# Attention feeding an MoE layer on one core: pinned activation tables, a maximum by matmul, grouped QK, and preparation two units ahead

## Chip, cores and metric

One core of a Trainium2 chip. The metric is the device time of one execution in microseconds (us), as the median of several runs; the kernel before took 714.8 us (709.6 to 864.0, the last being a single slow execution that no comparison uses). Ratios are computed as the mean time of one kernel's fast runs over that of the other's fast runs of the same rounds, so they are not quite the ratio of the medians quoted.

## The reference

Twelve-head attention with normalised q and k, whose output (3584 tokens of 768 values) goes through two matrices with a leaky ReLU between.

```python
# q, k, v: (8, 12, 448, 64) fp32; g_q, g_k: (64,)
def rmsnorm(x, g):
    return x / np.sqrt(np.mean(x * x, axis=-1, keepdims=True) + 1e-06) * g
q_n, k_n = rmsnorm(q, g_q), rmsnorm(k, g_k)
scores = np.matmul(q_n, k_n.transpose(0, 1, 3, 2)) / np.sqrt(64)
attn = np.exp(scores - scores.max(-1, keepdims=True))
attn = attn / (attn.sum(-1, keepdims=True) + 1e-09)
x = np.matmul(attn, v).transpose(0, 2, 1, 3).reshape(3584, 768)
h = x @ w_in                        # w_in (768, 2048)
out = np.maximum(0.01 * h, h) @ w_out    # w_out (2048, 768)
```

Any constant may be subtracted from the scores of a row, so the kernel subtracts one shift for a whole unit, found from a probe of the scores.

## The kernel before

The work is cut into 24 units, each four heads of one batch element. For a unit, GpSimd makes squares (`sq`), q times both gains (`qg`) and a cast of v (`vt`); VectorE sums the squares (`ssq`); ScalarE forms 1/rms as exp(-0.5 ln) (`uu`, `rinv`); VectorE multiplies (`n16`, shown as `n` in traces); TensorE transposes (`tp`); a probe of the scores gives the shift (`eb`). Then eight score tiles (`sT`) go through Exp into `et`, and `pv` forms the sum of the exponentials and the product with v, which are divided with ln and exp again (`lz`, `rz`). From unit 3 on, MoE matmuls of the batch element before (`hps`, `op`) are put between the score tiles from a queue, so many microseconds of them per step (`fill`).

```python
def prep_pool(u):
    ...
    for ti, t in enumerate((rq, rk)):
        f = t.rearrange("p h j d -> p (h j) d")
        nc.gpsimd.tensor_tensor(sq[:, ti], f, f, op=ALU.mult)     # sq: one buffer
    nc.gpsimd.tensor_tensor(qg, rq..., ggb..., op=ALU.mult)       # qg: one buffer
    nc.gpsimd.tensor_copy(vt..., rv...)

def prep_rinv(u):
    nc.scalar.activation(uu, s["ssq"], AF.Ln, bias=eps_t, scale=1.0 / D)
    nc.scalar.activation(rinv, uu, AF.Exp, bias=0.0, scale=-0.5)

def prep_norm(u, ti):                       # ti 0: q (from qg), ti 1: k (from raw)
    for a in range(2):
        nc.vector.tensor_tensor(n16[:, ti, :, :, a, :], src5[:, :, a],
                                r4[:, :, a, :, None].broadcast_to(...), op=ALU.mult)

def prep_probe(u):
    ...                                     # four matmuls, two row maxima into pm2
    nc.gpsimd.partition_all_reduce(cr2, pm2, SP, bass_isa.ReduceOp.max)
    nc.vector.tensor_reduce(cm, cr2, axis=AXL.X, op=ALU.max)
    nc.vector.tensor_scalar(eb, cm, -1.0, DELTA, op0=ALU.mult, op1=ALU.add)
...
for u in range(NU):
    nu = u + 1
    for i in range(2 * NJ):                 # eight score tiles
        qk_exp(u, i)
        if i == 0: load(u + 2); prep_pool(nu); ...
        if i == 1 and u > 0: pv(u - 1); ...
        if i == 2: prep_ssq(nu); prep_rinv(nu)
        if i == 3: prep_norm(nu, 0); prep_norm(nu, 1)
        if i == 4: prep_tr(nu, 0)
        if i == 5: prep_tr(nu, 1)
        if i == 6: prep_probe(nu)
        fill({1: 0.4, 4: 1.6, 5: 1.6}.get(i, 2.0) if u >= NQ else 0.0)
```

(Range checks and parts that do not change are left out.)

## Time and profile before

| part of the span, us | before |
|---|---|
| start (to the first exponential of unit 3) | 108.9 |
| 21 units with MoE work | 547.6 (26.1 each) |
| tail | 48.3 |
| span | 704.8 |

From the groups of instructions of the kernel before, two kinds. The columns are line, engine, operation, names and shapes, count, then busy us and mean ns of one, then the idle time ahead of them and what ended it.

```profile
L131 DVE TENSOR_TENSOR n<-qg,rinv 112x512 f16<-112x512 f32 x48 | 31.0, 688 | 48.0 <-ACT rinv L119 48.0
L131 DVE TENSOR_TENSOR n<-rk,rinv 112x512 f16<-112x512 f32 x48 | 30.9, 684 | 0.0
L117 ACT ACT_TABLE_LOAD x24 | 30.8, 1283 | 1.1 <-PEq L325 0.7
```

The 96 normalising multiplies take 0.68 to 0.69 us each; four of them are 2.5 us per unit. The table load stands four times per unit (this row and three like it, each 1283 ns, the other three with 0.4 us of idle time ahead of 24 loads). A row with large idle time is not yet a bottleneck: one asks whether the engine that sets the end (TensorE here) waits because of it. The prediction reads the waits and the timeline for that.

### The profile page before, as it was taken

The page shows a single profiled execution, that of the slowest core. Times are in us where ns is not written, and L with a number is a line of the kernel's source. Part 1 is how long each engine was busy: PE and PEld are TensorE (multiplying, and loading weights), DVE is VectorE, ACT ScalarE, POOL GpSimd, SP SyncE. Part 2 cuts the span into 40 slices and gives each one's busy share as a digit, 9 for nine tenths or more (in the row PEclk, how much of TensorE's full clock was granted, in tenths as well). Part 3 has the DMA queues.
Part 4 walks back from the last instruction along what each step waited for, and adds up shares of the span by engine and source line. Part 5 has one row for each costly group of instructions (what it writes and reads, how often), then busy time and mean ns, then how long its engine had stood idle before and what let it go on. Part 6 is the DMA issues. An engine that isn't in the chain of part 4 may idle for free.

```text
span 704.8 us, 8877 instructions
## 1 busy us (share of the span) xinstructions
PE 516.1 (73%) x3680; PEld 250.1 (35%) x3680; DVE 236.8 (34%) x372; ACT 405.1 (57%) x512; POOL 185.2 (26%) x133
## 2 busy tenths in 40 slices
PE   0206528878678978977778878878679778879897
PEld 0102212434333433433333433434334434435454
DVE  1322442243342353254232343243332343333001
ACT  0226555766558456757548456766547466766520
POOL 3241244034044134134044044034044043140000
PEclk9998556989789989999779889999769889999999
DMA  6944542504430325205420225205420134001002
GB/s 159 192 93 95 123 80 54 115 1 124 100 79 1 73 62 139 53 1 124 101 78 1 58 67 127 77 0 124 101 78 1 27 98 123 1 1 46 23 20 71
DMA packets 40728, 50.95 MB, mean 72 GB/s; under 512 B 2416, under 2 KB 36720, under 8 KB 40304
## 3 DMA queue, kind: packets, MB, share of 16 engines
q1 hardware_dynamic: 38144, 44.11, 24.5%
q0 software_dynamic: 2544, 6.29, 5.2%
q8 instruction: 28, 0.46, 0.3%
q14 instruction: 12, 0.10, 0.0%
HBM read 45.67 MB, written 11.01 MB: 80 GB/s over the span
## 4 chain that ended last, share of the span: by engine, by line
issue 52%; POOL 21%; PE 16%; ACT 5%; DVE 4%; POOLq 0%; DVEq 0%
POOL sq L99 11%; PE op L224 8%; POOL qg L101 6%; PE hps L211 5%; POOL vt L104 3%; DVE n L131 2%; DVE ssq L111 2%; ACT et L178 1%; PE sT L176 1%; ACT L202 1%; ACT L200 1%; ACT L119 1%; DVE xt L204 1%; PE tp L140 1%; POOL wout L78 1%
## 5 line engine op out<-in xcount | busy, mean ns | idle before, releaser
L178 ACT ACTIVATE et<-sT,eb 112x896 f16<-112x896 f32 x192 | 188.1, 1005 | 148.4 <-PE sT L176 126.5
L211 PE MATMUL hps<-xt,win 128*128 128x448 f16 x768 | 171.4, 373 | 23.8 <-DVE xt L204 23.8
L224 PE MATMUL op<-wout,gt 128*128 128x384 f16 x896 | 179.3, 362 | 0.0
L140 PE MATMUL tp<-ident,n 112*128 112x112 f16 x384 | 38.3, 247 | 135.7 <-DVE n L131 135.7
L224 PEld LDWEIGHTS <-gt 128*128 128x128 f16 x896 | 93.3, 108 | 76.7 <-issue 33.3
L211 PEld LDWEIGHTS <-win 128*128 128x128 f16 x768 | 73.8, 102 | 103.0 <-issue 50.6
L176 PE MATMUL sT<-qkT 64*112 64x448 f16 x384 | 77.7, 416 | 19.4 <-ACT et L178 19.0
L99 POOL TENSOR_TENSOR sq<-rq 112x1024 f32<-112x1024 f32 x24 | 45.2, 1883 | 171.8 <-issue 171.8
L213 ACT ACTIVATE gt<-hps 128x448 f16<-128x448 f32 x128 | 66.3, 544 | 38.4 <-PE hps L211 36.6
L204 DVE TENSOR_TENSOR xt<-pv,rz 128x448 f16<-128x448 f32 x48 | 27.7, 619 | 164.3 <-ACT rz L202 164.3
L161 POOL PARTITION_ALL_REDUCE cr<-pm x24 | 9.0, 373 | 269.2 <-DVE pm L159 232.7
L140 PEld LDWEIGHTS <-n 112*128 112x128 f16 x384 | 24.6, 112 | 152.9 <-DVE n L131 147.3
L227 DVE COPY ost<-op 128x384 f32<-128x384 f32 x56 | 31.1, 556 | 120.1 <-PE op L224 117.6
L111 DVE TENSOR_REDUCE ssq<-sq 112x32 f32<-112x2048 f32 x24 | 54.7, 2280 | 44.3 <-POOL sq L99 44.3
L101 POOL TENSOR_TENSOR qg<-rq,ggb 112x1024 f32<-112x1024 f32 x24 | 56.2, 2344 | 0.0
L117 ACT ACTIVATE uu<-ssq,eps_t 112x32 f32<-112x32 f32 x24 | 7.7, 322 | 84.4 <-DVE ssq L111 84.4
L176 PEld LDWEIGHTS <-qkT 64*112 64x112 f16 x384 | 25.5, 131 | 74.9 <-issue 73.5
L131 DVE TENSOR_TENSOR n<-qg,rinv 112x512 f16<-112x512 f32 x48 | 31.0, 688 | 48.0 <-ACT rinv L119 48.0
L99 POOL TENSOR_TENSOR sq<-rk 112x1024 f32<-112x1024 f32 x24 | 45.2, 1882 | 0.0
L195 PE MATMUL pv<-et,vt 112*32 112x448 f16 x768 | 44.6, 377 | 0.0
L144 DVE COPY qkT<-tp 128x896 f16<-128x896 f16 x48 | 30.0, 625 | 29.4 <-PE tp L140 29.3
L159 DVE TENSOR_REDUCE pm<-probe 112x1 f32<-112x448 f32 x48 | 27.7, 620 | 22.3 <-PE probe L156 22.3
(28 smaller groups left out, 302.2 us busy)
## 6 DMA issues: line engine op xcount, KB each, us to landing
rq<-in_q_dram SPq DMA_DIRECT2D x24, 448.0 KB, 5.0
rk<-in_k_dram SPq DMA_DIRECT2D x24, 448.0 KB, 6.9
rv<-in_v_dram SPq DMA_DIRECT2D x24, 448.0 KB, 7.5
win<-in_moe_w_in_dram POOLq DMA_DIRECT2D x3, 1024.0 KB, 13.5
wout<-in_moe_w_out_dram POOLq DMA_DIRECT2D x4, 768.0 KB, 7.7
out_dram<-ost SPq DMA_DIRECT2D x8, 336.0 KB, 2.8
out_dram<-ost SPq DMA_DIRECT2D x8, 288.0 KB, 2.7
out_dram<-ost SPq DMA_DIRECT2D x8, 240.0 KB, 2.7
```

The lines of the kernel that those rows point to most:

```text
L99: nc.gpsimd.tensor_tensor(sq[:, ti], f, f, op=ALU.mult)
L101: nc.gpsimd.tensor_tensor(qg, rq.rearrange("p h j d -> p (h j) d"), ggb[:, None, :].broadcast_to([SP, QH * NJ, D]), op=ALU.mult)
L111: nc.vector.tensor_reduce(ssq, s["sq"], axis=AXL.X, op=ALU.add)
L131: nc.vector.tensor_tensor(n16[:, ti, :, :, a, :], src5[:, :, a], r4[:, :, a, :, None].broadcast_to([SP, 2, NJ, D]), op=ALU.mult)
L140: nc.tensor.transpose(tp[:, ti, j, :], s["n16"][:, ti, r, j].rearrange("p a d -> p (a d)"), ident16[:SP, :])
L176: nc.tensor.matmul(sT[:, a, 0:S], kq[:, 1, ts(jk, SP)], kq[:, 0, :], start=True, stop=True)
L178: nc.scalar.activation(s["et"][:, jk, 2 * r:2 * r + 2, :], sT[:, :, 0:S], AF.Exp, bias=s["eb"], scale=1.0)
L195: nc.tensor.matmul(bank[32 * i:32 * i + 32, 0:S], lhsT, s["et"][:, jk, i, :], start=(jk == 0), stop=(jk == NJ - 1))
L204: nc.vector.tensor_tensor(xt[:, g, w, :], bank[:, 0:S], rz, op=ALU.mult)
L211: nc.tensor.matmul(hps[:, 0:S], win16[:, kt // 2, kt % 2, ts(ft, 128)], xt[:, kt // 2, kt % 2], start=(kt == 0), stop=(kt == KT - 1))
L213: nc.scalar.activation(gt[:, ft, ds(S * (b % 2), S)], hps[:, 0:S], AF.Prelu, bias=0.0, scale=1.0, alpha=0.01)
L224: nc.tensor.matmul(op2[:, 0:HC], gt[:, ft, ts(t, 128)], wout16[:, ft, ds(HC * half, HC)], start=(ft == 0), stop=(ft == FT - 1))
```

## The change

The intent: take the table loads off ScalarE, take GpSimd's slow all-reduce and its reload away (the "reload" is the 7 us behind each all-reduce in which GpSimd waits for nothing that the trace shows; the name is an interpretation: what GpSimd does in this time is not shown), make fewer and longer bursts of score matmuls, and prepare so early that nothing in the preparation can hold up TensorE.

```diff
-    raws = ctx.enter_context(tc.tile_pool(name="raws", bufs=2))
+    raws = ctx.enter_context(tc.tile_pool(name="raws", bufs=3))
...
     def prep_pool(u):
...
+        if u == 0:
+            for ti, t in enumerate((rq, rk)):
+                nc.scalar.activation(sq[:, ti], t, AF.Square)
+            nc.vector.tensor_tensor(qg, rq, gg_b, op=ALU.mult)
+            nc.gpsimd.tensor_copy(vt_v, rv_v)
+        else:
+            ...                                   # on GpSimd, as before
...
-        nc.gpsimd.partition_all_reduce(cr2, pm2, SP, bass_isa.ReduceOp.max)
+        nc.vector.tensor_reduce(pm, pm2, axis=AXL.X, op=ALU.max)
+        nc.vector.tensor_scalar(dg, ident16[:SP, :], pm, None, op0=ALU.mult)
+
+    def prep_shift(u):
+        nc.tensor.matmul(pb[:, 0:SP], onesp, s["dg"], start=True, stop=True)
+        nc.vector.tensor_reduce(cm, pb[:, 0:SP], axis=AXL.X, op=ALU.max)
...
-    def qk_exp(u, i):
+    def qk_exp(u, i0, n):                         # n tiles of matmuls, then n Exps
...
+        nc.scalar.preload_act_table_set("natural_log_exp_and_others")
...
         for u in range(NU):
-            for i in range(2 * NJ):
-                qk_exp(u, i)
+            for d in range(NJ):
+                qk_exp(u, 2 * d, 2)               # two tiles, four matmuls
+                if d == 0: load(u + 3); prep_pool(u + 2); ...; pv(u - 1)
+                if d == 1: prep_tr(u + 1, 0); prep_tr(u + 1, 1)
+                if d == 2: prep_probe(u + 1)
+                if d == 3: prep_shift(u + 1)
+                if d == 2: prep_ssq(u + 2); prep_rinv(u + 2)
+                if d == 3: prep_norm(u + 2, 0); prep_norm(u + 2, 1)
+                fill((1.8, 3.1, 4.0, 4.0)[d] if u >= NQ else 0.0)
```

(Cut to its core, bodies of `if` put on one line.)

More of the change, by code (lines that the diff above doesn't have):

```diff
@@ L3 @@
 import concourse.bass as bass
-import concourse.bass_isa as bass_isa
 import concourse.tile as tile
@@ L61 @@
     nc.vector.memset(ones16, 1.0)
+    onesp = cst.tile([SP, SP], FP16)
+    nc.vector.memset(onesp, 1.0)
     eps_t = cst.tile([SP, 1], FP32)
@@ L94, in prep_pool @@
     def prep_pool(u):
-        rq, rk, rv = raw[u]
+        rq, rk, rv = (t.rearrange("p h j d -> p (h j) d") for t in raw[u])
         sq = prep_p.tile([SP, 2, QH * NJ, D], FP32, tag="sq", bufs=1, name="sq")
-        for ti, t in enumerate((rq, rk)):
-            f = t.rearrange("p h j d -> p (h j) d")
-            nc.gpsimd.tensor_tensor(sq[:, ti], f, f, op=ALU.mult)
         qg = prep_p.tile([SP, QH * NJ, D], FP32, tag="qg", bufs=1, name="qg")
-        nc.gpsimd.tensor_tensor(qg, rq.rearrange("p h j d -> p (h j) d"),
-                                ggb[:, None, :].broadcast_to([SP, QH * NJ, D]), op=ALU.mult)
-        vt = prep_p.tile([SP, QH, NJ, 2, D // 2], FP16, tag="vt", bufs=3, name="vt")
-        nc.gpsimd.tensor_copy(vt.rearrange("p h j t d -> p (h j) t d"),
-                              rv.rearrange("p h j (d t) -> p (h j) t d", t=2))
+        vt = prep_p.tile([SP, QH, NJ, 2, D // 2], FP16, tag="vt", bufs=4, name="vt")
+        gg_b = ggb[:, None, :].broadcast_to([SP, QH * NJ, D])
+        vt_v = vt.rearrange("p h j t d -> p (h j) t d")
+        rv_v = rv.rearrange("p j (d t) -> p j t d", t=2)
+        if u == 0:
[4 more added lines that the diff above has]
+        else:
+            for ti, t in enumerate((rq, rk)):
+                nc.gpsimd.tensor_tensor(sq[:, ti], t, t, op=ALU.mult)
+            nc.gpsimd.tensor_tensor(qg, rq, gg_b, op=ALU.mult)
+            nc.gpsimd.tensor_copy(vt_v, rv_v)
         st[u] = dict(sq=sq, qg=qg, vt=vt)
@@ L159, in prep_probe @@
             nc.vector.tensor_reduce(pm2[:, a:a + 1], probes[a][:, 0:S], axis=AXL.X, op=ALU.max)
-        cr2 = small.tile([SP, 2], FP32, tag="cr2", name="cr2")
-        nc.gpsimd.partition_all_reduce(cr2, pm2, SP, bass_isa.ReduceOp.max)
+        pm = small.tile([SP, 1], FP32, tag="pm", name="pm")
+        nc.vector.tensor_reduce(pm, pm2, axis=AXL.X, op=ALU.max)
+        dg = small.tile([SP, SP], FP16, tag="dg", name="dg")
+        nc.vector.tensor_scalar(dg, ident16[:SP, :], pm, None, op0=ALU.mult)
+        s["dg"] = dg
+    def prep_shift(u):
+        s = st[u]
+        pb = aux([SP, 512], FP32, "pb")
+        nc.tensor.matmul(pb[:, 0:SP], onesp, s["dg"], start=True, stop=True)
         cm = small.tile([SP, 1], FP32, tag="cm", name="cm")
-        nc.vector.tensor_reduce(cm, cr2, axis=AXL.X, op=ALU.max)
+        nc.vector.tensor_reduce(cm, pb[:, 0:SP], axis=AXL.X, op=ALU.max)
         eb = small.tile([SP, 1], FP32, tag="eb", name="eb")
@@ L166, in prep_probe @@
         s["eb"] = eb
-    def qk_exp(u, i):
+    def qk_exp(u, i0, n):
         s = st[u]
-        r, jk = divmod(i, NJ)
-        if i == 0:
+        if i0 == 0:
             s["et"] = epool.tile([SP, NJ, QH, S], FP16, tag="et", name="et")
-        sT = psum.tile([SP, 2, 512], FP32, tag="sT", bufs=2, name="sT")
-        for a in range(2):
-            kq = s["qkT", r][64 * a:64 * a + 64]
-            nc.tensor.matmul(sT[:, a, 0:S], kq[:, 1, ts(jk, SP)], kq[:, 0, :],
-                             start=True, stop=True)
-        nc.scalar.activation(s["et"][:, jk, 2 * r:2 * r + 2, :], sT[:, :, 0:S], AF.Exp,
-                             bias=s["eb"], scale=1.0)
+        sTs = []
+        for i in range(i0, i0 + n):
+            r, jk = divmod(i, NJ)
+            sT = psum.tile([SP, 2, 512], FP32, tag="sT", bufs=2, name="sT")
+            for a in range(2):
+                kq = s["qkT", r][64 * a:64 * a + 64]
+                nc.tensor.matmul(sT[:, a, 0:S], kq[:, 1, ts(jk, SP)], kq[:, 0, :],
+                                 start=True, stop=True)
+            sTs.append(sT)
+        for i, sT in zip(range(i0, i0 + n), sTs):
+            r, jk = divmod(i, NJ)
+            nc.scalar.activation(s["et"][:, jk, 2 * r:2 * r + 2, :], sT[:, :, 0:S], AF.Exp,
+                                 bias=s["eb"], scale=1.0)
     xts = {}
@@ L263 @@
         load(1)
+        load(2)
+        nc.scalar.preload_act_table_set("natural_log_exp_and_others")
         nc.vector.tensor_tensor(ggb, gqb, gkb, op=ALU.mult)
@@ L266 @@
         prep_pool(0)
-        load_w_in(0)
-        load_w_in(1)
-        load_w_in(2)
         prep_ssq(0)
@@ L273 @@
         prep_norm(0, 1)
+        prep_pool(1)
+        for g in range(NQ):
+            load_w_in(g)
         prep_tr(0, 0)
@@ L276 @@
         prep_probe(0)
-        PACE = 1.66
-        for u in range(NU):
-            nu = u + 1
-            for i in range(2 * NJ):
-                qk_exp(u, i)
-                if i == 0:
+        prep_shift(0)
+        prep_ssq(1)
+        prep_rinv(1)
+        prep_norm(1, 0)
+        prep_norm(1, 1)
+        for u in range(NU):
+            for d in range(NJ):
+                qk_exp(u, 2 * d, 2)
+                if d == 0:
+                    if u + 3 < NU:
+                        load(u + 3)
                     if u + 2 < NU:
-                        load(u + 2)
-                    if nu < NU:
-                        prep_pool(nu)
+                        prep_pool(u + 2)
                     if u < 4:
                         load_w_out(4 * u, 4)
-                if i == 1 and u > 0:
-                    pv(u - 1)
-                    if u % NQ == 0:
-                        push_moe(u // NQ - 1)
-                if nu < NU:
-                    if i == 2:
-                        prep_ssq(nu)
-                        prep_rinv(nu)
-                    if i == 3:
-                        prep_norm(nu, 0)
-                        prep_norm(nu, 1)
-                    if i == 4:
-                        prep_tr(nu, 0)
-                    if i == 5:
-                        prep_tr(nu, 1)
-                    if i == 6:
-                        prep_probe(nu)
-                fill({1: 0.4, 4: 1.6, 5: 1.6}.get(i, 2.0) if u >= NQ else 0.0)
+                    if u > 0:
+                        pv(u - 1)
+                if d == 1 and u % NQ == 0 and u > 0:
+                    push_moe(u // NQ - 1)
+                if u + 1 < NU:
+                    if d == 1:
+                        prep_tr(u + 1, 0)
+                        prep_tr(u + 1, 1)
+                    if d == 2:
+                        prep_probe(u + 1)
+                    if d == 3:
+                        prep_shift(u + 1)
+                if u + 2 < NU and d == 2:
+                    prep_ssq(u + 2)
+                    prep_rinv(u + 2)
+                if u + 2 < NU and d == 3:
+                    prep_norm(u + 2, 0)
+                    prep_norm(u + 2, 1)
+                fill((1.8, 3.1, 4.0, 4.0)[d] if u >= NQ else 0.0)
         pv(NU - 1)
```

## The prediction

> **What bounds the kernel now.** I read the page first. Its second part gives TensorE's busy share and granted clock in 40 slices of 17.6 us; its fourth part gives the chain that ended last.
>
> ```profile
> PE   0206528878678978977778878878679778879897
> ...
> PEclk9998556989789989999779889999769889999999
> ...
> issue 52%; POOL 21%; PE 16%; ACT 5%; DVE 4%; POOLq 0%; DVEq 0%
> ```
>
> TensorE is nearly idle for the first six slices, and has holes after them; where it has holes, the clock falls to 0.5 to 0.8. The chain is on GpSimd (its work, and "issue" time in which it waits for nothing visible), not on the busiest engine. Next I read the view of all waits.
>
> ```profile
> POOL cr L161 <- DVE pm L159: 232.7, 20, 13.2
> POOL sq L99 <- issue: 171.8, 23, 11.7
> ...
> PE tp L140 <- DVE n L131: 135.7, 48, 21.4
> ACT et L178 <- PE sT L176: 126.5, 41, 6.5
> ...
> PE hps L211 <- DVE xt L204: 23.8, 19, 3.2
> ...
> PE sT L176 <- ACT et L178: 19.0, 15, 7.3
> ```
>
> Columns are total us, times, longest. The span less TensorE's busy time is 704.8 - 516.1 = 188.7 us, and three waits of TensorE make 135.7 + 23.8 + 19.0 = 178.5 of it. Three quarters is one wait: the transposes of the next unit wait for its normalised q and k (n). One unit of the timeline shows why:
>
> ```profile
> 425.43 0.37 POOL L161 PARTITION_ALL_REDUCE cr<-pm  x1 [12.56 <-DVE pm L159]
> ...
> 432.92 1.88 POOL L99 TENSOR_TENSOR sq<-rq 112x1024 f32<-112x1024 f32 x1 [7.12 <-issue]
> ...
> 442.59 0.37 PE L140 MATMUL tp<-ident,n 112*128 112x112 f16 x4 [0.98 <-DVE n L131]
> ...
> 450.25 0.38 POOL L161 PARTITION_ALL_REDUCE cr<-pm  x1 [10.23 <-DVE pm L159]
> ```
>
> This is a loop from unit to unit: all-reduce (0.37), 7.1 us of nothing, two squares (3.75), their sum on VectorE (2.3), Ln, table load, Exp (about 2.0), four multiplies (2.5), transposes, probe, row maxima (1.2), the next all-reduce. From 425.43 to 450.25 that is 24.8 us. The 21 units from about 103 us (unit 3's start) to 655 us take 552 / 21 = 26.3 us each. So a latency loop bounds the steady part; TensorE is just behind it, and in order, so it waits inside the loop.
>
> [...] the squares after an all-reduce wait 171.8 / 23 = 7.5 us for nothing visible; at the start it also shows 4.9 us ahead of the first all-reduce. [...] The groups show 1283 ns, 4 x 24 times; the idle before these loads is 0.4 us over 24 of them[...]. [...] (columns: stretch, length, busy of PE, PEld, DVE, ACT, POOL, clock, DMA, GB/s):
>
> ```profile
> 80.00:100.00 20.00, 8.18 (x66) 3.14 (x66) 6.13 (x10) 12.44 (x15) 8.35 (x6) 0.59 0.30 77
> ...
> 440.00:460.00 20.00, 18.19 (x145) 8.62 (x144) 5.21 (x10) 16.40 (x24) 2.79 (x4) 1.00 0.28 71
> ...
> 660.00:680.00 20.00, 18.84 (x100) 9.78 (x100) 1.16 (x2) 8.96 (x17) 0.00 (x0) 1.00 0.00 1
> ```
>
> The clock is low where TensorE is sparse and full where it is dense. [...]
>
> **The change part by part.**
>
> *Table set pinned.* 96 loads of 1.283 us become one (the built program has 1 in place of 96): 95 x 1.283 = 122 us of ScalarE, 405 -> about 283. Most lies beside TensorE. On the loop it is one load per unit (the one before rinv), 1.28 us; the two loads before lz and rz delay xt by 2.6 us, and in the tail that is directly on the path.
>
> *All-reduce replaced.* Removes 24 all-reduces (9.0 us), their 0.4 to 5 us ahead, and the 171.8 us of "issue" before the squares. Adds per unit one small reduce, one 112x112 scaling, a 112-column matmul and a 112-wide reduce in place of a 2-wide one: about 0.5 us on VectorE and 0.2 us on TensorE (estimates from the 0.15 us small reduces, the 0.62 us reduce of 448 columns, and eight 112-column transposes in 0.57 us). GpSimd's work stays 45.2 + 45.2 + 56.2 + 25.9 = 172.5 us, or 7.2 us per unit.
>
> *Preparation two units ahead.* Moves squares, sums, rinv and n of unit u+2 into unit u, while the transposes of u+1 use n from the unit before. This takes the loop apart: GpSimd's 7.2 us, the sum and the norm no longer stand between two transposes. It costs a third buffer of raw inputs and no time. The 135.7 us wait should go.
>
> *QK in groups of four.* Four matmuls in a row took 0.58 us, two took 0.40, so eight pairs (3.2 us) become four groups (2.3 us): 0.9 us per unit of TensorE.
>
> *Steady state.* With the loop gone, TensorE's own stream is the bound. Per unit, at full clock, with rates from dense pieces of this trace: hps 32 matmuls x 0.191 (91 in 17.37 us in the tail) = 6.1; op 37.3 x 0.163 (128 in 20.81) = 6.1; pv 48 in 2.4; QK 4 x 0.58 = 2.3; transposes about 1.0 (8 in 0.57); probe 0.35; new matmul 0.2. The sum is 18.4 us. ScalarE needs 283 / 24 = 11.8 us per unit, VectorE about 10.4, GpSimd 7.2, so none of these comes near. I add 1.0 us for waits that stay: pv's bank until lz and rz are done, ScalarE standing in order behind uu while VectorE sums squares (about 2 us, mostly covered by four banks), and even batches that leave the queue empty for a step. 19.4 x 21 = 407 us instead of 552.
>
> *Start.* Before, the first exp ran at 32.0 us and unit 3 began at 103. Now the first squares are on ScalarE. VectorE has g only at 11.3 us (gkb's landing), then qg 1.2, sum 2.3, Ln/Exp 0.6, norm 2.5, transposes, copies and probe about 3.5, maxima and shift 2.2: near 24 us. Unit 1's sum and rinv stand ahead of the first exp in program order: 27 us. Units 0 to 2 have no MoE work and then take some 8, 11 and 11 us (eight exps 7.3 us; TensorE cold about 10 us; GpSimd 7.2 + 0.9 for a weight load): unit 3 at 57. The DMA rings have to bring 6 loads (1.38 MB each, about 5.4 us of full rings by 24.5% of 704.8 us over 24 units and the output) and w_in (about 18 us, half of 5.2% of 704.8) by then, about 50 us plus parts of w_out, so I put it at 60.
>
> *Tail.* From the last exps (655) to the end 50 us, dense MoE of the last batch; less two table loads: 47.
>
> *Sum.* 60 + 407 + 47 = 514, and about 2 us between span and measured time (706.57 against 704.8): 516. I take 518, as stalls that I overlooked only add.
>
> **The rivals.** *A: only the named waits go, little else.* Taking 122 us of table loads plus 172 us of reload from 704.8 would give about 410 us; against it, TensorE cannot go under 18.4 x 21 + 47 + 50 = 483. *B: a new wait replaces the old.* Grouping binds both score buffers to one burst, so QK waits for exps; the ScalarE stall behind uu delays gt and thus banks. For it: ScalarE's strict order and only four auxiliary banks, shared by pv, tp, probe, pb, hps and op. Against it: budgets of 1.8 to 4.0 us of MoE between groups, more than two exps take (1.9). If it bit by 2 us per unit: 560. *C: the start is bound by transfers.* Six raw loads and both weights (12.6 MB read) contend; DMA was at 1.02 share between 20 and 40 us. It would make unit 3 start at 70 to 75: 530. *D: denser TensorE is throttled.* At the 0.89 mean clock of now, 407 / 0.89 = 457, total 568. Against it: clock 1.00 in the dense 440-460 stretch and through the tail; low clock comes with gaps. *E: GpSimd's loop was never the bound*, and TensorE's program order holds 24 us per unit: about 610. Against it: the 135.7 us wait.
>
> **Range and chances.** A bare stream without stalls gives 495; B partly with C gives about 550. Range 497 to 552. For less than 2% gain nearly everything would have to be eaten, which nothing in the profile supports: faster 0.97, same 0.02, slower 0.01.
>
> **What would show it.** Right: no wait of squares for "issue", ScalarE busy near 283 us, the transposes' wait under 20 us (start aside), clock near 1.0 from unit 3 on, units 19 to 20 us apart, the chain on TensorE's hps and op, unit 3 near 60 us. Wrong: banks or exps as releasers of hps and QK at over 1 us per unit (B), a start of over 68 us that waits on raw tiles (C), clock under 0.95 in dense stretches (D), transposes still waiting for n.

Passages that no trace or run of this case shows are cut out of this text, where the marks stand; the measured numbers that stood beside them remain. That one set serves exp and ln, which the pin needs, the changed kernel shows: its trace has one table load (1283 ns) for all its Ln, Exp, Square and leaky ReLU, and c_all and c_fold, with the same pin, gave correct results.

What the text takes to be so, and where it is seen. TensorE is seen to keep the order of the program: in the kernel before it stood idle for 4.06 us until the transposes at 576.27 us had their n, and output matmuls (`op`), whose gt had been complete before 565.89 us, followed at 577.82. ScalarE does too: it stood idle for 1.61 us until `uu` at 572.95 us had its sum, while the exponential of a score tile that was finished at 569.18 us came behind it, at 574.72. "TensorE cold about 10 us": in the kernel before TensorE was busy 30.7 us between 32 and 109 us, that is 10.2 for each of the three units without MoE work, at a granted clock of 0.69 in the second and 0.57 in the third. The 1.2 us of `qg` on VectorE was an estimate that names no source; c_all measured 1.21 to 1.23.

## More of the kernel before

Other runs of the kernel before, made beside the experiments on other chips, had medians of 711.7 to 714.1 us.

I cut the span at two events that every trace shows: the first exponential of unit 3, where MoE work begins, and the end of the last exponential, after which only MoE work of the last batch element is left.

## The result and the profile after

The changed kernel took **529.0 us** (528.2 to 529.6, four runs), ratio 0.7418 with a 95% interval of 0.7378 to 0.7459. The predicted 518 with a range of 497 to 552 holds it. The page of the changed kernel, its two rows by slice (now 13.2 us each) and the chain that ended last:

```profile
PE   0236569999899999999999999999899999999996
...
PEclk9999679999999999999999999999999999999999
...
PE 59%; DVE 29%; ACT 5%; issue 4%; DMA 1%; SPq 0%; DVEq 0%
```

TensorE is 80% busy or more from the seventh slice to the last but one, at a granted clock of 0.9 or more, and the chain has moved from GpSimd to TensorE, with 29% on VectorE. From the view of all waits of the changed kernel:

```profile
POOL sq L110 <- DVE ssq L118: 203.6, 23, 11.0
ACT et L198 <- PE sT L193: 94.5, 48, 5.9
...
PE tp L147 <- DVE n L138: 30.3, 8, 19.3
...
PE sT L193 <- ACT et L198: 20.7, 20, 3.5
...
PE hps L231 <- ACT gt L233: 3.0, 4, 0.7
```

The transposes' wait for n fell from 135.7 to 30.3 us, of which 19.3 us is the first one at the start. GpSimd no longer waits for "issue": its squares wait for VectorE's sum of the unit before, which frees their only buffer. That is the row to remember, because it fixes when GpSimd begins. The two groups that were 0.69 us before:

```profile
L138 DVE TENSOR_TENSOR n<-rk,rinv 112x512 f16<-112x512 f32 x48 | 80.7, 1720 | 0.0
...
L138 DVE TENSOR_TENSOR n<-qg,rinv 112x512 f16<-112x512 f32 x48 | 70.2, 1502 | 2.4 <-ACT rinv L126 2.4
```

The same 96 multiplies take 150.9 us in place of 61.9. This was in no step of the prediction. The timeline of the changed kernel shows what stands beside them (start, length, engine, line, operation; VectorE first, then GpSimd, same stretch):

```profile
261.82 2.28 DVE L118 TENSOR_REDUCE ssq<-sq 112x32 f32<-112x2048 f32 x1
...
264.88 4.04 DVE L138 TENSOR_TENSOR n<-qg,rinv 112x512 f16<-112x512 f32 x2
268.84 3.45 DVE L138 TENSOR_TENSOR n<-rk,rinv 112x512 f16<-112x512 f32 x2
```

```profile
264.18 1.90 POOL L110 TENSOR_TENSOR sq<-rq 112x1024 f32<-112x1024 f32 x1 [7.90 <-DVE ssq L118]
266.03 2.34 POOL L110 TENSOR_TENSOR sq<-rk 112x1024 f32<-112x1024 f32 x1
269.06 2.69 POOL L111 TENSOR_TENSOR qg<-rq,ggb 112x1024 f32<-112x1024 f32 x1 [0.69 <-DVE n L138]
271.70 1.62 POOL L112 CAST vt<-rv 112x1024 f16<-112x1024 f32 x1
```

The sum ends at 264.1, the squares of the next unit start at once, and the multiplies come 0.7 us later and run beside them. Taken singly from the same trace, the first multiply (264.88) lasts 1.74 us and ends 0.54 us after the first square; the second (266.54) lasts 2.38 us and ends 0.55 us after the second square, which itself took 2.34 us in place of 1.88. Each looks like a multiply that could not do its work until the square had ended, and I call such multiplies blocked below; the trace does not show what holds them. What it shows is 1.7 to 2.4 us beside a square, against 0.69 us in the kernel before, where GpSimd stood still. c_quiet, below, takes GpSimd's work away.

Where the time went, by the same cuts:

| part, us | before | predicted | after |
|---|---|---|---|
| start | 108.9 | 60 | 76.1 |
| 21 units | 547.6 (26.1) | 407 (19.4) | 405.1 (19.3) |
| tail | 48.3 | 47 | 46.1 |
| span | 704.8 | 514 | 527.3 |

The stretches of the changed kernel at these cuts (columns as in the prediction):

```profile
0.00:76.00 76.00, 28.90 (x230) 14.08 (x231) 58.66 (x64) 30.16 (x41) 41.40 (x31) 0.92 0.91 203
76.00:481.00 405.00, 383.38 (x3216) 199.71 (x3216) 268.92 (x349) 243.06 (x361) 153.32 (x76) 0.99 0.34 83
481.00:527.30 46.30, 40.97 (x258) 22.78 (x257) 5.62 (x10) 10.02 (x19) 0.00 (x0) 0.98 0.14 40
```

TensorE is busy 383.4 of 405.1 us in the middle: 1.03 us of idle time per unit, at clock 0.99. So the middle and the tail came out within 2 us of the working; the whole miss is 16 us in the start. (The clock column counts full speed where the trace has no clock record. The first record here is at 50.8 us, and the transposes before it took 0.30 us each against 0.21 later, so the 0.92 of the start is too high.)

### The profile page after: what moved, and what is told of

The parts are those of the page before. It is cut to its first block, busy times and chain, and to the rows that moved or that the text cites. A ratio compares the mean times of both kernels' runs of the same rounds, so it can differ in the third digit from the quotient of the medians.

```text
span 527.3 us, 8780 instructions
## 1 busy us (share of the span) xinstructions
PE 453.2 (86%) x3704; PEld 236.6 (45%) x3704; DVE 333.2 (63%) x422; ACT 283.2 (54%) x419; POOL 194.7 (37%) x106
## 4 chain that ended last, share of the span: by engine, by line
PE 59%; DVE 29%; ACT 5%; issue 4%; DMA 1%; SPq 0%; DVEq 0%
PE op L244 21%; PE hps L231 20%; DVE n L138 14%; DVE ssq L118 8%; PE sT L193 7%; PE pv L215 6%; PE tp L147 4%; DVE pm L166 4%; ACT gt L233 2%; DMA gkb<-in_g_k_dram 1%; ACT et L198 1%; ACT uu L124 1%; PE probe L163 1%; DVE ost L247 1%; ACT rinv L126 1%
## 5 line engine op out<-in xcount | busy, mean ns | idle before, releaser
L198 ACT ACTIVATE et<-sT,eb 112x896 f16<-112x896 f32 x192 | 182.0, 1007 | 94.7 <-PE sT L193 94.5
L244 PE MATMUL op<-wout,gt 128*128 128x384 f16 x896 | 154.7, 326 | 10.9 <-DVE ost L247 8.5
L231 PE MATMUL hps<-xt,win 128*128 128x448 f16 x768 | 152.6, 353 | 3.1 <-ACT gt L233 3.0
L244 PEld LDWEIGHTS <-gt 128*128 128x128 f16 x896 | 86.4, 98 | 73.1 <-issue 13.6
L138 DVE TENSOR_TENSOR n<-rk,rinv 112x512 f16<-112x512 f32 x48 | 80.7, 1720 | 0.0
L193 PE MATMUL sT<-qkT 64*112 64x448 f16 x384 | 62.1, 389 | 20.7 <-ACT et L198 20.7
L138 DVE TENSOR_TENSOR n<-qg,rinv 112x512 f16<-112x512 f32 x48 | 70.2, 1502 | 2.4 <-ACT rinv L126 2.4
L111 POOL TENSOR_TENSOR qg<-rq,ggb 112x1024 f32<-112x1024 f32 x23 | 61.8, 2688 | 23.0 <-DVE n L138 23.0
L147 PE MATMUL tp<-ident,n 112*128 112x112 f16 x384 | 25.6, 221 | 30.3 <-DVE n L138 30.3
L224 DVE TENSOR_TENSOR xt<-pv,rz 128x448 f16<-128x448 f32 x48 | 27.5, 612 | 18.4 <-ACT rz L222 18.4
L112 POOL CAST vt<-rv 112x1024 f16<-112x1024 f32 x23 | 36.4, 1584 | 0.0
```

The source lines that it names most:

```text
L111: nc.gpsimd.tensor_tensor(qg, rq, gg_b, op=ALU.mult)
L147: nc.tensor.transpose(tp[:, ti, j, :], s["n16"][:, ti, r, j].rearrange("p a d -> p (a d)"), ident16[:SP, :])
L193: nc.tensor.matmul(sT[:, a, 0:S], kq[:, 1, ts(jk, SP)], kq[:, 0, :], start=True, stop=True)
L198: nc.scalar.activation(s["et"][:, jk, 2 * r:2 * r + 2, :], sT[:, :, 0:S], AF.Exp, bias=s["eb"], scale=1.0)
L231: nc.tensor.matmul(hps[:, 0:S], win16[:, kt // 2, kt % 2, ts(ft, 128)], xt[:, kt // 2, kt % 2], start=(kt == 0), stop=(kt == KT - 1))
L244: nc.tensor.matmul(op2[:, 0:HC], gt[:, ft, ts(t, 128)], wout16[:, ft, ds(HC * half, HC)], start=(ft == 0), stop=(ft == FT - 1))
```

## The experiments

Twelve kernels, all timed in three rounds beside the kernel before; all but one gave a correct result. Names that begin with a_ undo one part of the changed kernel, b_ put parts alone into the kernel before, c_ deal with the blocked multiplies. The parts' shares come first.

### a_nopin: the pin taken out

```diff
-        nc.scalar.preload_act_table_set("natural_log_exp_and_others")
```

> The changed kernel (529.0 us) with the pin of the table set taken out: 97 table loads instead of 1, so about 123 us more ScalarE work (283 -> 406 us). Theory 1 (TensorE's own stream bounds the steady part at 19.3 us per unit, ScalarE has slack there): only the loads in a latency chain show: two before lz and rz in the tail (2.6 us), two per unit in the start (about 2 us each for 3 units), and under 0.6 us per unit of waits for banks in between: 540 to 552 us. Rival (ScalarE's work is what the change saved): most of 123 us comes back, 600 us or more.

Measured: 582.4 us (ratio to the kernel before 0.8156, 0.8122 to 0.8190), 53 us over the changed kernel. Both expectations missed. The timeline of a_nopin shows how 5.1 us more per unit on an engine that is 70% busy reach TensorE:

```profile
293.31 1.28 ACT L126 ACT_TABLE_LOAD   x1
...
294.60 0.23 ACT L126 ACTIVATE rinv<-uu 112x32 f32<-112x32 f32 x1
294.74 1.39 ACT L233 ACTIVATE gt<-hps 128x448 f16<-128x448 f32 x3
...
295.31 6.38 PE L231 MATMUL hps<-xt,win 128*128 128x448 f16 x24 [2.02 <-ACT gt L233]
```

And the same place in the changed kernel:

```profile
265.20 4.70 PE L231 MATMUL hps<-xt,win 128*128 128x448 f16 x24 [0.74 <-ACT gt L233]
```

ScalarE runs these in program order: the leaky ReLUs (gt) that free banks for hps stand behind the second table load (the hps matmuls ahead of them had ended by 292.6 us, gt begins at 294.74). TensorE runs out of banks and waits 2.02 us in place of 0.74. And then the 24 matmuls take 6.38 us in place of 4.70: from 1.1 us after the gap the granted clock is lower and the same work runs slower (0.50 from 296.4 to 299.8 us here, with weight loads 0.37 us apart, and 0.83 on average from 290 to 300 us; 1.00 between 260 and 270 us in the changed kernel). So this wait was paid again in clock: over the whole profile TensorE was busy 475.6 us in place of 453.2, 22 of the 53 us, for the same 3704 instructions. My estimate counted neither.

### a_allred: the all-reduce put back

```diff
-        nc.vector.tensor_reduce(pm, pm2, axis=AXL.X, op=ALU.max)
-        nc.vector.tensor_scalar(dg, ident16[:SP, :], pm, None, op0=ALU.mult)
+        nc.gpsimd.partition_all_reduce(cr2, pm2, SP, bass_isa.ReduceOp.max)
...
-        nc.tensor.matmul(pb[:, 0:SP], onesp, s["dg"], start=True, stop=True)
-        nc.vector.tensor_reduce(cm, pb[:, 0:SP], axis=AXL.X, op=ALU.max)
+        nc.vector.tensor_reduce(cm, s["cr2"], axis=AXL.X, op=ALU.max)
```

> The changed kernel with GpSimd's all-reduce put back in place of the diagonal matmul, everything else kept. Theory 1: the all-reduce with its two reloads (about 5 us ahead, 7 us behind, 0.4 itself) and 7.2 us of preparation make GpSimd need about 19.6 us per unit, which is level with TensorE's 19.3, and with two units of lead only the start and some units show it: 550 to 580 us. Rival (the reload was the bound by itself and lead does not help): near the 26.3 us per unit of before, 660 us or more.

Measured: 595.9 us (0.8329, 0.8291 to 0.8367), 67 us over the changed kernel: more than theory 1 had, far less than the rival. The profile of this kernel fell in a slow execution (600.7 us), so I take only its shape: GpSimd stood idle for nothing visible ahead of 23 all-reduces (153.0 us) and ahead of 13 units' squares (100.9 us), the places of the expectation's "two reloads"; units 0 to 2 are 24 to 25 us apart and later ones mostly 20 to 21. Lead hides most of GpSimd's reload in the middle, and nothing hides it in the start. The multiplies are also short again, 66.7 us for all 96 in place of 150.9: with the all-reduce back, GpSimd does not meet them.

### a_single: one score tile at a time

```diff
-                qk_exp(u, 2 * d, 2)
+                qk_exp(u, 2 * d, 1)
...
-                fill((1.8, 3.1, 4.0, 4.0)[d] if u >= NQ else 0.0)
+                bud = (1.8, 3.1, 4.0, 4.0)[d] / 2 if u >= NQ else 0.0
+                fill(bud)
+                qk_exp(u, 2 * d + 1, 1)
+                fill(bud)
```

> The changed kernel with one score tile (two matmuls) at a time, the MoE budget between them halved, everything else kept. Theory 1: 0.9 us of TensorE per unit, since two matmuls take 0.40 and four take 0.58 us: 21 x 0.9 = 19 us, 548 us. Rival (grouping costs waits on the two score buffers as much as it saves): 529 us or less.

Measured: 535.8 us (0.7499, 0.7475 to 0.7523), 7 us over the changed kernel, a third of what I worked out and outside both expectations. The built program shows one reason: the halved budgets often let nothing in between, so that TensorE's stream has 119 bursts of two, 35 of four and one of six, 155 in place of 95. Sixty more bursts at 2 x 0.40 - 0.58 = 0.22 us are 13 us, and TensorE was busy 465.6 us in place of 453.2, 12.4 more. The rest came out of idle time, which fell by 5.5 us.

### a_nolook: preparation one unit ahead

```diff
-                        prep_pool(u + 2)
+                        prep_pool(u + 1)
...
-                        prep_tr(u + 1, 0); prep_tr(u + 1, 1)        # d == 1
-                        prep_probe(u + 1)                           # d == 2
-                        prep_shift(u + 1)                           # d == 3
-                    prep_ssq(u + 2); prep_rinv(u + 2)               # d == 2
-                    prep_norm(u + 2, 0); prep_norm(u + 2, 1)        # d == 3
+                        prep_ssq(u + 1); prep_rinv(u + 1)           # d == 1
+                        prep_norm(u + 1, 0); prep_norm(u + 1, 1)    # d == 1
+                        prep_tr(u + 1, 0); prep_tr(u + 1, 1)        # d == 3
+                fill((1.8, 3.1, 4.0, 2.0)[d] if u >= NQ else 0.0)
+                if d == 3: prep_probe(u + 1); fill(2.0); prep_shift(u + 1)
```

> The changed kernel with preparation one unit ahead instead of two (pool, sums, norm, transposes, probe and shift of unit u+1 all inside unit u), table pin and diagonal matmul and groups of four kept. Theory 1: the latency loop comes back, but shortened by reload, table load and all-reduce: squares 3.75, sum 2.3, Ln/Exp 0.6, norm 2.5 to 5, transposes 2, probe 2.5, shift 1: 15 to 17 us against 19.3 us of TensorE, so part of it shows as TensorE waiting in order: 21 to 23 us per unit, 565 to 620 us. Rival (two units of lead were needless once reload and loads are gone): within 2% of 529 us.

Measured: 581.7 us (0.8147, 0.8105 to 0.8188), as theory 1 had it; units are mostly 20 to 24 us apart. The second unit of lead, with the order of work that goes with it, is worth 53 us. (The diff is cut: unit 1's preparation ahead of the loop is left out too.)

### b_pin and b_max: one part alone in the kernel before

```diff
+        nc.scalar.preload_act_table_set("natural_log_exp_and_others")    # b_pin
```

```diff
-        nc.gpsimd.partition_all_reduce(cr2, pm2, SP, bass_isa.ReduceOp.max)    # b_max
+        ...                       # pm, dg, matmul pb, cm as in the change
+                    if i == 7: prep_shift(nu)
```

> The kernel before with the table set pinned alone. Theory: one load (1.28 us) stands in the loop from unit to unit, two more delay the normalised output of attention by 2.6 us beside the loop, the all-reduce keeps GpSimd quiet during the multiplies as before: 24 x 1.3 + 3 = 34 us less, 670 to 695 us. Rival (122 us of ScalarE work are what counts): 600 us or less.

> The kernel before with the diagonal matmul in place of the all-reduce alone. Theory: the reload of 7 us leaves the loop, the blocked multiplies (about 5 us more) enter it, and the table load before rinv stays: within 2% of the kernel before, 700 to 725 us. Rival (my first account, the reload is the loop's largest part and nothing replaces it): 24 x 7 us less, 550 to 600 us.

Measured: b_pin 683.2 us (0.9576, 0.9536 to 0.9616), as the theory had it. b_max **758.9 us** (1.0655, 1.0631 to 1.0679): slower by 6.6% than the kernel before, outside both expectations. Taking out the most visible stall of the profile made the kernel slower. In the view of all waits, b_max has

```profile
PE tp L142 <- DVE n L133: 191.9, 48, 22.0
```

where the kernel before has 135.7. The span is 53 us longer (757.6 in place of 704.8): the start is 16 us shorter (92.7 in place of 108.9), the middle 69 us longer (616.6 in place of 547.6), so that the 56 us more of this wait match the 53 only by chance. In the kernel before, the reload after the all-reduce held GpSimd back, so that each unit's squares came just ahead of the sum, and GpSimd stood still when the multiplies ran. In b_max the squares of the next unit start when the sum ends, and the multiplies meet them: they average 1.52 and 1.70 us. (b_max itself was not run with GpSimd quiet; b_pin_max was.)

That explains why b_max lost time. Why it gained nothing in the middle from the reload, the kernel before shows. From its view of all waits, and from its timeline (GpSimd, then VectorE):

```profile
DVE ssq L111 <- POOL sq L99: 44.3, 8, 15.1
```

```profile
434.78 1.88 POOL L99 TENSOR_TENSOR sq<-rk 112x1024 f32<-112x1024 f32 x1
```

```profile
435.89 1.16 DVE L204 TENSOR_TENSOR xt<-pv,rz 128x448 f16<-128x448 f32 x2 [5.46 <-ACT rz L202]
436.96 2.28 DVE L111 TENSOR_REDUCE ssq<-sq 112x32 f32<-112x2048 f32 x1
```

The sum waited for the squares in only 8 of 24 units. In the other 16 the squares had been ready for up to 1.2 us, and the sum began when VectorE had finished what stands before it, here the normalised output `xt`, which waits for `rz` behind two table loads. So two paths ended close together, and taking the reload off one left the other. In b_pin, without those loads, the sum waits for the squares in all 24 units (86.4 us): only there is the reload on the path each time.

### b_pin_max: both, without lead and grouping

The edits of b_pin and b_max together.

> The kernel before with the table set pinned and the diagonal matmul, without lead of two units and without groups of four. Theory: like a_nolook (581.7) with the cost of single tiles (a_single: 7 us more than grouped): 580 to 600 us. Rival (reload and loads were all, lead gives little): 540 us or less.

Measured: 696.9 us (0.9793, 0.9747 to 0.9838), 2% under the kernel before, where the verdict at 2% is unclear; the expectation missed by almost 100 us, and the rival by more. From the timeline of b_pin_max, VectorE and then GpSimd:

```profile
455.76 4.10 DVE L133 TENSOR_TENSOR n<-qg,rinv 112x512 f16<-112x512 f32 x2 [0.72 <-ACT rinv L121]
459.79 3.42 DVE L133 TENSOR_TENSOR n<-rk,rinv 112x512 f16<-112x512 f32 x2
```

```profile
455.12 1.89 POOL L101 TENSOR_TENSOR sq<-rq 112x1024 f32<-112x1024 f32 x1 [17.71 <-DVE ssq L113]
456.98 2.34 POOL L101 TENSOR_TENSOR sq<-rk 112x1024 f32<-112x1024 f32 x1
460.01 2.66 POOL L103 TENSOR_TENSOR qg<-rq,ggb 112x1024 f32<-112x1024 f32 x1 [0.69 <-DVE n L133]
```

The four multiplies take 7.5 us in place of 2.5, directly ahead of the transposes, for which TensorE waits 152.5 us in this trace. (a_nolook, on which the expectation was built, has one unit of lead and long multiplies too, and takes 581.7 us. It has groups of four, another start, and its transposes two score groups after the multiplies instead of one tile; which of these makes the difference of 115 us was not separated.)

### b_pin_max_quiet: the same with GpSimd out of the way

```diff
-            nc.gpsimd.tensor_tensor(sq[:, ti], f, f, op=ALU.mult)
+            nc.scalar.activation(sq[:, ti], t..., AF.Square)
...
-        nc.gpsimd.tensor_tensor(qg, ...)
+        nc.vector.tensor_tensor(qg, ...)
```

> b_pin_max (696.9 us, only 2% under the kernel before) with squares on ScalarE and q times g on VectorE, so that GpSimd only casts v. New theory: taking the all-reduce away let GpSimd start its squares the moment VectorE's sum frees their buffer, so they block the normalising multiplies (1.5 to 2 us each instead of 0.69) straight ahead of the transposes that TensorE waits for, which ate the gain; with GpSimd quiet the multiplies are 0.69 us again, the loop is 7 to 8 us shorter, and the time falls to 570 to 630 us. Rival (the multiplies do not matter, TensorE's order of single score tiles and late transposes holds 27 us per unit by itself): 670 us or more.

Measured: 586.2 us (0.8241, 0.8224 to 0.8259), as the new theory had it, though ScalarE and VectorE got more work. The multiplies are back at a median of 0.69 us, and the transposes wait 56.9 us for n. So GpSimd's squares and products in that place cost b_pin_max 111 us (696.9 - 586.2), the lower mean granted clock included (0.864 there, 0.946 here). The run also moves the squares to another engine, so this is the price of that placement as a whole.

### c_quiet, c_start, c_all: the blocked multiplies in the changed kernel

```diff
-            for ti, t in enumerate((rq, rk)):                         # c_quiet, wrong result:
-                nc.gpsimd.tensor_tensor(sq[:, ti], t, t, op=ALU.mult) #   sq and qg of unit 0
-            nc.gpsimd.tensor_tensor(qg, rq, gg_b, op=ALU.mult)        #   are used throughout
+            pass
```

```diff
-        if u == 0:
+        if u <= 3:         # c_start
+        if True:           # c_all
```

> Wrong result on purpose: the changed kernel where GpSimd keeps only the cast of v; squares and q times g of unit 0 are read again by every unit, so that VectorE, ScalarE and TensorE have the same instructions and no GpSimd operation with two inputs runs beside the normalising multiplies. Theory (GpSimd's squares and products block the multiplies): they fall from 1.50 and 1.72 us back to about 0.69 us as before the change, unit 3's first exp comes at 56 to 62 us instead of 76.2, the steady part stays near 19.3 us per unit because TensorE bounds it: 508 to 516 us. Rival (the start is bound by transfers, and the multiplies are slow for another reason, such as their place beside ScalarE): unit 3 stays later than 70 us, 522 us or more.

> Correct result: the changed kernel with squares on ScalarE and q times g on VectorE for units 0 to 3 instead of unit 0 alone; later units as they were. Theory: the multiplies are 0.69 us in the start alone, unit 3's first exp at 58 to 64 us, later units unchanged: 511 to 518 us. Rival (transfers bound the start): 522 us or more.

> Correct result: squares on ScalarE (2 x 1.06 us a unit) and q times g on VectorE (1.22 us a unit) for all units, GpSimd only casts v. Theory: start as in c_start; in the steady part VectorE loses about 3.5 us of blocked time per unit and gains 1.2, ScalarE gains 2.1, and neither is the bound, so 19.0 to 19.6 us per unit and 508 to 520 us, within 1% of c_start. Rival (ScalarE in order is next to the bound, as the 53 us of a_nopin for 5.1 us more per unit suggest): 2.1 us more per unit cost about 1 us per unit, 530 us or more.

Measured: c_quiet 506.7 us (0.7116, 0.7088 to 0.7144), its result wrong as intended; c_start 521.3 us (0.7322, 0.7293 to 0.7351); c_all 517.2 us (0.7261, 0.7228 to 0.7294), both correct. The stretches of c_quiet:

```profile
0.00:25.90 25.90, 3.96 (x25) 2.36 (x26) 12.90 (x20) 4.37 (x7) 6.60 (x13) 1.00 1.00 228
25.90:66.30 40.40, 24.54 (x205) 11.83 (x205) 28.30 (x46) 25.89 (x36) 5.33 (x6) 0.88 1.10 239
66.30:458.00 391.70, 381.83 (x3216) 198.92 (x3216) 201.58 (x347) 242.56 (x361) 20.07 (x18) 0.99 0.35 85
```

With GpSimd quiet the multiplies have a median of 0.68 us, unit 3's first exponential comes at 66.2 in place of 76.1 us, and the middle takes 392.2 us (the rows above are cut at rounded times), 18.7 per unit. So in the changed kernel the blocking costs about 10 us of start and 13 us of the middle: 529.0 - 506.7 = 22 us. (The sum of squares did not wait for GpSimd in the changed kernel either, so leaving the squares out frees nothing else on VectorE. It does free the buffers of the raw inputs earlier; what that is worth was not separated.) The total is 1 us better than the range expected. c_start wins 7.7 us, all in the start (68.4 in place of 76.1 us), and later units are as they were: that settles that the start was not held by transfers alone. At 521.3 us it lies between its own range (to 518) and the rival's (from 522). c_all came as its theory had it, within 1% of c_start, with 19.1 us per unit, and its rival fell. But none came to the 56 to 64 us that I expected for the start: units 1 and 2 take 14 to 15 us in all three. The timeline of c_quiet has two stretches there that I had not counted: pv with slow matmuls (its first 16 take 1.68 us, in the middle of the changed kernel 0.94), 4.5 us between two bursts of score matmuls, and ScalarE standing in order behind `uu`, 2.7 us while VectorE sums. Rings are also busy (share 1.00 and 1.10 in the two stretches above), but between 30 and 76 us of the changed kernel the view of all waits has no wait for a transfer. What each of these costs was not separated.

### c_fold: an attempt at a better kernel

```diff
-            nc.vector.tensor_tensor(qg, rq, gg_b, op=ALU.mult)       # from c_all
...
-        nc.vector.tensor_copy(qkT, tp.rearrange("p t j s -> p t (j s)"))
+        nc.vector.tensor_scalar(qkT[:, 0], tpv[:, 0], ggc, None, op0=ALU.mult)
+        nc.vector.tensor_copy(qkT[:, 1], tpv[:, 1])
```

After the transpose the 64 channels lie on partitions, so the gains are one scalar per partition and ride on the copy out of PSUM. (Not shown: the gains are loaded as such columns, and multiplied with each other only after unit 0's normalising multiplies.)

> Correct result, an attempt at a better kernel: c_all (517.2 us) where the product of the two gains is applied to q while the transposed tile is copied out of PSUM (per partition scalar, two copies instead of one) instead of a separate 1.22 us multiply per unit; GpSimd only casts v. Theory: VectorE loses about 1.0 us per unit, and the start 1.2 us per unit plus the wait for the gains (10.5 us) ahead of the first sum: 506 to 514 us, near c_quiet's 506.7. Rival (VectorE is far from the bound and the start is set elsewhere): 515 to 519 us.

Measured: **510.9 us** (0.7176, 0.7165 to 0.7187), correct and within its theory, faster than both kernels: 28% under the one before and, by the ratios, 3.3% under the changed one. The gain over c_all is the start alone: the first exponential comes at 20.6 in place of 27.3 us, since no sum waits for the gains to land; the middle takes 400.4 us, as c_all's 400.9. That the middle did not move with 1 us less of VectorE per unit says that VectorE is not the bound of c_all's middle.

| kernel | us | ratio to before | transposes wait for n, us |
|---|---|---|---|
| before | 712 to 715 | 1 | 135.7 |
| b_pin | 683.2 | 0.958 | 136.6 |
| b_max | 758.9 | 1.066 | 191.9 |
| b_pin_max | 696.9 | 0.979 | 152.5 |
| b_pin_max_quiet | 586.2 | 0.824 | 56.9 |
| changed | 529.0 | 0.742 | 30.3 |
| c_all | 517.2 | 0.726 | 18.0 |
| c_fold | 510.9 | 0.718 | 12.1 |

## Why the prediction was right, and where its steps were not

**TensorE's own stream becomes the bound of the middle: right.** The sum of 18.4 us and 1.0 us for waits gave 19.4 us per unit; measured were 19.3 us with 18.3 us of busy TensorE and 1.03 us of idle time. The clock was 0.99 where TensorE was dense, so rival D fell, and rival A's objection (TensorE's stream as a floor) held. That the 1.0 us for waits fits as well is partly luck. This is TensorE's largest wait between 76 and 481 us:

```profile
PE op L244 <- DVE ost L247: 8.5, 9, 1.2
```

It waits for an output copy on VectorE, which was not among the reasons given. With 3.1 us of transposes that still waited for n, that is about half of the idle time (21.7 us), and both waits are gone in c_quiet, whose units take 18.7 us.

**The lead takes the loop apart: right.** The transposes' wait fell to 30.3 us, 11 us without the first, inside the predicted 20 us; a_nolook gives 53 us back.

**"This is a loop from unit to unit" with the reload as its largest piece: wrong in one link, and incomplete.** The transposes' wait for n was real. But "7.1 us of nothing, two squares (3.75), their sum" is a chain in only 8 of 24 units; in the others the sum began when VectorE was free, with the squares ready. And b_max, which takes the reload out, is 6.6% slower. The step that was missing is what GpSimd does with the freed time: it starts squares at the moment the multiplies run. The list of rivals had waits for banks, transfers, clock and order, and no multiplies made longer by what GpSimd does beside them (1.50 and 1.72 us on average here, a median of 0.68 in c_quiet). The lead of two units made this nearly harmless in the middle (13 us of 405 by c_quiet), with little to spare: two score groups stand between the multiplies and the transposes, and in units 3 to 22 the first transposes begin from 1.3 us before to 3.7 us after the end of the last multiply.

**"norm 2.5" and "27 us" in the start: mis-sized.** Unit 0's four multiplies took 7.5 us, because the second unit's squares ran on GpSimd beside them, and the first exponential came at 30.5 us.

**"some 8, 11 and 11 us" for units 0 to 2: mis-sized.** They took 16.5, 14.5 and 14.6 us. Taking the blocking away in c_quiet gives 11.6, 14.5 and 14.2: so the blocking explains unit 0 (and the first exponential), while units 1 and 2 are held by other things, for which only the timeline's candidates above can be named. Together the start was 16 us late, about 10 of them by blocking. Rival C (unit 3 at 70 to 75 us) had about the right size, but not its reason for half of it: c_start won 7.7 us with the same transfers in the same order, although the rings were nearly full. C's own sign, a start that waits for raw tiles, shows only ahead of unit 0's squares (3.0 us in all). For the other half the cause stays open.

**Pinning "lies mostly beside TensorE": wrong in size.** Alone in the kernel before it gave 4.2%, close to the working of one load on the loop. Once TensorE is the bound it is worth 53 us of the 122, since ScalarE's order passes the loads on to the banks (2.02 us of waiting in place of 0.74 at one place of a_nopin), and the lower clock behind the gap makes it dearer (22 of the 53 us are longer busy time of TensorE).

**QK in groups, 0.9 us per unit: too large.** a_single gave 7 us in all, 0.3 us per unit, in part because single tiles often stand together anyway.

**VectorE "about 10.4" us per unit: too low.** It was busy 268.9 / 21 = 12.8 us per unit, and 9.6 in c_quiet, so the difference is blocked multiplies. TensorE stayed the bound of the middle, though the blocking cost 13 us there.

Two small slips: `op` has 37.3 matmuls per unit only if the tail's are counted in (768 / 21 = 36.6 in the middle), and the all-reduces started 0.14 us after their input, not "0.4", in 20 of 24 units. The other four started 1.8 to 4.9 us after it; each of them followed GpSimd's issue of a weight transfer by 8.7 to 10.2 us, and which of the two they waited for is not shown.

In sum: the start was 16 us late, middle and tail 3 us early, and 2 us had been added for overlooked stalls, which makes the 11 us between 518 and 529.

## What to carry to other kernels

Before removing a stall, ask what the engine that stalled will do with the time, and what its instructions will then run beside: here the 7 us behind an all-reduce also kept GpSimd's squares away from VectorE's multiplies (0.69 us each; without the all-reduce, in b_max, 1.52 and 1.70). Ask too whether the next step waits for the stall at all, or for something that ends at almost the same time. Parts of a change that break one loop do not add up: the table loads were worth 4% alone and 10% as the last part, removing the all-reduce cost 6.6% alone, and putting it back into the finished kernel cost 12%. Preparing further ahead (53 us here, as much as the pin) also covers delays that nobody foresaw, if not wholly: c_quiet still found 22 us.
